# Reordering the start of a transformer block: the third tile's norm first, transposes inside a half step, scale groups inside the K steps

## The chip, the core and the metric

The kernel runs on one core of one Trainium2 chip. The metric is the device time of one execution in microseconds (us), measured in several executions; medians are quoted. A profile is one execution recorded instruction by instruction. Its span is 1.7 to 2 us shorter than the quoted time of an execution, so only differences are compared across the two.

TensorE does the matmuls. VectorE and ScalarE do elementwise work and copy results out of PSUM, the memory that matmuls write. GpSimd does a few small operations. The sync queue issues the loads, which 16 DMA engines carry out. In profile lines PE is TensorE, PEld its weight loads, DVE VectorE, ACT ScalarE, POOL GpSimd and SP the sync queue; L280 is a line of the kernel, x6 a count, `out<-in` names tiles: `pk` the K accumulators, `pq` those of q, `pt` transposes, `pm` scale factors, `big` the modulated rows.

## The reference

One block of a diffusion transformer, with 2 batches of 256 rows and a width D of 1152. All inputs are bf16.

```python
mod = (_silu(c) @ w_mod).reshape(B, 6, 1, D)
shift_a, scale_a, gate_a, shift_m, scale_m, gate_m = [mod[:, i] for i in range(6)]
h = _layernorm(x, axis=-1) * (1 + scale_a) + shift_a
qkv = (h @ wqkv).reshape(B, N, 3, H, Dh)
# ... softmax attention with two heads, output projection wo ...
x = x + gate_a * a
h2 = _layernorm(x, axis=-1) * (1 + scale_m) + shift_m
m = _gelu(h2 @ w_fc1) @ w_fc2
return x + gate_m * m
```

The change concerns the first 26 us: the first layer norm, `scale_a`, and the K part of `qkv`.

## The kernel before

The 512 rows are four tiles of 128: tiles 0 and 1 are batch 0, tiles 2 and 3 are batch 1. The width is nine chunks of 128. For each chunk k, TensorE transposes the normalized rows (`transpose_x`). VectorE scales batch 0's half on its way out of PSUM and ScalarE scales batch 1's half (`both`, called modulation here). Six matmuls of 512 columns then add chunk k into six K accumulators (`k_step`). The factors `scale_a` of a pair of chunks come from a scale group: 9 matmuls of 2 columns per chunk, then one add of 1.0 on VectorE (`scale_add`).

```python
def both(pt, k):
    for b, e in enumerate("da"):                 # d: VectorE, a: ScalarE
        modulate(pt, 0, k, b, b * N, e)
# ... statistics of tile 0 on ScalarE, of tile 1 on VectorE; both rstd ...
act_stats(2)                                     # tile 2: two passes on ScalarE
stats_piece(3, 0)                                # tile 3: three pieces on VectorE
stats_piece(3, 1)
norm1(1, 0, CUT)
norm1(0, 0, CUT)
pt_a = transpose_x([0, 1], BT[0])
fill(1)                                          # a matmul nobody reads: keeps TensorE busy
stats_piece(3, 2)
pool_eps(3)
pool_rsqrt(3, 4)
act_mean_eps(2)
act_root(2)
root_exp(2, 3)
pm0, pm1 = [scale_group(k, k + 1, acc_tile) for k in range(2)]
nc.vector.tensor_scalar_mul(hT0[:, 0, 0:N], pt_a[:, 0, :], pm0[:, 0, 0:1])
# ... batch 0's other modulation ...
norm1(3, 0, CUT)
norm1(2, 0, CUT)
fill(1)
k_step(0, 0, N)                                  # batch 0's half steps
k_step(1, 0, N)
pt_c = aux_tile([P, 2, N], "pt", BF16)
transpose_x([0, 1], [3], pt_c, 1)
transpose_x([0, 1], [2], pt_c, 0)
modulate(pt_c, 0, 0, 1, 0, "d")
modulate(pt_c, 1, 1, 1, 0, "a")
# ...
k_step(0, N, T)                                  # batch 1's first half step
# ... steps 1 and 2 ...
for k in range(3, KD):
    split = 2 if k == 5 else 0
    k_step(k, 0, T, 0, split)                    # the step's first `split` matmuls
    if k in (3, 5, 7):
        k1 = min(k + 3, KD)
        scale_add(scale_group(k + 1, k1), k + 1, k1)
    if k < KD - 1:
        both(transpose_x([k + 1], range(NT)), k + 1)
    k_step(k, 0, T, split)                       # the rest of the step
```

After step 8 come three more K panels (`k_panel`), then q, the scores, v, the output projection, and the two big matmuls fc1 and fc2.

Of the kernel before, what the change touches and what calls it, by code (L numbers as in the profile page):

```python
# [9 lines left out]
BF16 = mybir.dt.bfloat16  # L10
# [9 lines left out]
def kernel(  # L20
# [12 lines left out]
    B, N, D = x.shape  # L33
# [3 lines left out]
    P = 128  # L37
    T = B * N
    NT = T // P
    TPB = N // P  # L40
    KD = D // P
# [3 lines left out]
    NPD = D // PW  # L45
# [14 lines left out]
    def acc_tile(shape, name, dt=FP32):  # L60
        return psum.tile(shape, dt, name=name, tag="acc", bufs=6)

    def aux_tile(shape, name, dt=FP32):
        return psum.tile(shape, dt, name=name, tag="aux", bufs=2)
# [127 lines left out]
    def stats_piece(t, j):  # L192
        nc.vector.bn_stats(stats1[t][:, j, :], x_sb[:, t, j * PW:(j + 1) * PW])
        if j == NPD - 1:
            nc.vector.bn_aggr(mv1[:, t, :], stats1[t][:].rearrange("p a b -> p (a b)"))
# [8 lines left out]
    def act_stats(t):  # L204
        for f, dst in ((ACT.Identity, dsum), (ACT.Square, dsq)):
            nc.scalar.activation(
                sink[:], x_sb[:, t, :], f, bias=x_sb[:, t, 0:1], scale=-1.0,
                accum_out=dst[:, t:t + 1],
            )
# [22 lines left out]
    def norm1(t, c0, c1):  # L232
        nc.vector.tensor_scalar(
            xns[t][:, c0:c1], x_sb[:, t, c0:c1], mv1[:, t, 0:1], rstd1[:, t:t + 1],
            op0=ALU.subtract, op1=ALU.mult,
        )
# [4 lines left out]
    def scale_group(k0, k1, tile_of=aux_tile):  # L241
        pm = tile_of([P, k1 - k0, B], "pm")
        for j in range(k0, k1):
            if j == 0:
                nc.tensor.matmul(pm[:, 0, :], ones_row[:], ones_row[:, 0:B], start=True, stop=False)
            for k in range(KD):
                nc.tensor.matmul(
                    pm[:, j - k0, :], w_scale_a[:, k, j * P:(j + 1) * P], sT[:, k, 0:B],
                    start=(k == 0 and j > 0), stop=(k == KD - 1),
                )  # L250
        return pm

    def scale_add(pm, k0, k1, eng="d"):
        if eng == "a":
            nc.scalar.activation(scale_a[:, k0:k1, :], pm[:], ACT.Identity, bias=ones[:])
        else:
            nc.vector.tensor_scalar_add(scale_a[:, k0:k1, :], pm[:], 1.0)

    def transpose_x(ks, ts, pt=None, j0=0):
        if pt is None:  # L260
            pt = aux_tile([P, len(ks), len(ts) * P], "pt", BF16)
        for j, t in enumerate(ts, j0):
            for i, k in enumerate(ks):
                nc.tensor.transpose(pt[:, i, j * P:(j + 1) * P], xns[t][:, k * P:(k + 1) * P], ident[:])
        return pt

    def modulate(pt, i, k, b, j0, eng):
        dst, src, sc = hT0[:, k, b * N:(b + 1) * N], pt[:, i, j0:j0 + N], scale_a[:, k, b:b + 1]
        if eng == "d":
            nc.vector.tensor_scalar_mul(dst, src, sc)  # L270
        else:
            nc.scalar.mul(dst, src, sc)
# [3 lines left out]
    def k_step(k, c0=0, c1=T, m0=0, m1=KM1):  # L276
        for m in range(m0, m1):
            if k == 0 and c0 == 0:
                pk[m] = acc_tile([P, T], "pk")
            nc.tensor.matmul(  # L280
                pk[m][:, c0:c1], w_k[:, k, m * P:(m + 1) * P], hT0[:, k, c0:c1],
                start=(k == 0 and c0 == 0), stop=(k == KD - 1), skip_group_check=True,
            )
# [30 lines left out]
    CUT = 4 * P  # L314
    BT = [range(b * TPB, (b + 1) * TPB) for b in range(B)]

    def both(pt, k):
        for b, e in enumerate("da"):
            modulate(pt, 0, k, b, b * N, e)

    def fill(n):
        for _ in range(n):
            nc.tensor.matmul(pwarm[:], zeros[:, 0:P], zeros[:], start=True, stop=True)

    def pool_eps(t):
        nc.gpsimd.tensor_scalar_add(mv1[:, t, 1:2], mv1[:, t, 1:2], LN_EPS)

    def pool_rsqrt(t0, t1):
        nc.gpsimd.tensor_tensor(
            rstd1[:, t0:t1], mv1[:, t0:t1, 1:2].rearrange("p t o -> p (t o)"),  # L330
            neg_half[:, 0:t1 - t0], op=ALU.pow,
        )

    def act_root(t):
        nc.scalar.activation(rstd1[:, t:t + 1], dsq[:, t:t + 1], ACT.Ln, bias=dm2[:, t:t + 1], scale=1.0 / D)

    def root_exp(t0, t1):
        nc.scalar.activation(rstd1[:, t0:t1], rstd1[:, t0:t1], ACT.Exp, scale=-0.5)

    def act_mean_eps(t):  # L340
        act_sq_mean(t)
        nc.gpsimd.tensor_scalar_add(dm2[:, t:t + 1], dm2[:, t:t + 1], LN_EPS)
        act_mean(t)
# [7 lines left out]
    nc.scalar.activation(rstd1[:, 1:2], mv1[:, 1, 1:2], ACT.Ln, bias=eps_t[:], scale=1.0)  # L351
    root_exp(0, 2)
    act_stats(2)
    stats_piece(3, 0)
    stats_piece(3, 1)
    norm1(1, 0, CUT)
    norm1(0, 0, CUT)
    pt_a = transpose_x([0, 1], BT[0])
    fill(1)
    stats_piece(3, 2)  # L360
    pool_eps(3)
    pool_rsqrt(3, 4)
    act_mean_eps(2)
    act_root(2)
    root_exp(2, 3)
    pm0, pm1 = [scale_group(k, k + 1, acc_tile) for k in range(2)]
    nc.vector.tensor_scalar_mul(hT0[:, 0, 0:N], pt_a[:, 0, :], pm0[:, 0, 0:1])
    nc.vector.tensor_copy(scale_a[:, 0:1, :], pm0[:])
    scale_add(pm1, 1, 2)
    modulate(pt_a, 1, 1, 0, 0, "d")  # L370
    norm1(3, 0, CUT)
    norm1(2, 0, CUT)
    fill(1)
    k_step(0, 0, N)
    k_step(1, 0, N)
    pt_c = aux_tile([P, 2, N], "pt", BF16)
    transpose_x([0, 1], [3], pt_c, 1)
    transpose_x([0, 1], [2], pt_c, 0)
    modulate(pt_c, 0, 0, 1, 0, "d")
    modulate(pt_c, 1, 1, 1, 0, "a")  # L380
    norm1(0, CUT, D)
# [13 lines left out]
    k_step(2, 0, N)  # L395
    k_step(2, N, T)
    for k in range(3, KD):
        split = 2 if k == 5 else 0
        k_step(k, 0, T, 0, split)
        if k in (3, 5, 7):  # L400
            k1 = min(k + 3, KD)
            scale_add(scale_group(k + 1, k1), k + 1, k1)
        if k < KD - 1:
            both(transpose_x([k + 1], range(NT)), k + 1)
        k_step(k, 0, T, split)
    for m in range(KM1):
        k_evac(m)
# [386 lines left out]
    for gi, (n, t, c0, cw) in enumerate(groups):  # L794
# [3 lines left out]
        for kk in range(KF):  # L798
            j, r = divmod(n * KF + kk, 27)
# [55 lines left out]
```

## Time and profile before

The time before was 243.84 us (three runs, 243.69 to 244.43). From the page of the kernel before, the busy time of TensorE, and then, in 40 equal slices of the span, the busy tenths of the DMA engines and the rate:

```profile
PE 236.7 (98%) x1699; PEld 144.9 (60%) x1699; DVE 91.2 (38%) x193; ACT 60.0 (25%) x121; POOL 28.1 (12%) x47
...
DMA  6999999997579999239999999999300000000000
GB/s 210 318 317 294 378 367 391 389 392 241 124 252 399 387 382 182 47 58 334 392 390 392 345 326 302 273 326 289 94 20 16 20 16 16 19 18 17 27 23 16
```

TensorE is nearly always busy, and for the first 50 us the DMA engines are busy too, so either might set the pace there. The chain of waits, followed back from the last instruction, gives one candidate. Columns: start us, us, what ("issue" is time in which nothing that the profile shows was waited for).

```profile
18.62 1.66 SPq L129
...
20.32 12.40 DMA w_q<-in_wqkv_dram
32.72 0.05 issue
32.77 5.35 PE pq L522 x24
```

q's first matmul started when the first load of `w_q` landed, at 32.72 us. The waits of TensorE from 8 to 36 us (who waited, for what, us in total, times, longest) are these three:

```profile
PE pm L247 <- DMA w_scale_a<-in_w_mod_dram: 0.5, 1, 0.5
PE pk L280 <- DVE big L270: 0.4, 1, 0.4
PE pq L522 <- DMA w_q<-in_wqkv_dram: 0.2, 1, 0.2
```

The first is the wait for the first scale factors, the second the wait before batch 1's first K matmul, and the third the wait before q. The timeline around step 4 (first two lines) and around steps 7 and 8 shows what the change moves in the loop (start us, us, engine, line, operation, out<-in, shapes, count, idle before):

```profile
17.68 0.39 PE L264 MATMUL pt<-ident,xn 128*128 128x128 bf16 x4
17.91 1.89 PE L280 MATMUL pk<-big,w_k 128*128 128x512 bf16 x8
...
22.74 0.37 PE L247 MATMUL pm<-sT,w_scale_a 128*128 128x2 bf16 x9
...
22.97 0.38 PE L264 MATMUL pt<-ident,xn 128*128 128x128 bf16 x4
...
23.14 0.16 DVE L257 TENSOR_SCALAR scale_a<-pm 128x2 f32<-128x2 f32 x1 [1.20 <-PE pm L247]
23.19 2.75 PE L280 MATMUL pk<-big,w_k 128*128 128x512 bf16 x12
23.41 0.35 DVE L270 TENSOR_SCALAR big<-pt,scale_a 128x256 bf16<-128x256 bf16 x1
...
23.79 0.47 ACT L272 ACTIVATE big<-pt,scale_a 128x256 bf16<-128x256 bf16 x1 [1.34 <-DVE big L270]
```

Step 4's matmuls follow the transposes ahead of them (4 x 56 ns) without a hole. For step 8, the scale group and the transposes come first. Then the six matmuls of step 7 and the six of step 8 run as one row of 12, 2.75 us, while the add, VectorE and ScalarE prepare step 8 behind them.

**How holes are measured below.** From start to start, a matmul of 512 columns takes 216 ns in this trace when the next one is ready, one of 256 columns 109 ns, a transpose 56 ns, and a 2-column matmul 25 ns. A hole is the time from start to start above that pace. By this measure batch 1's first K matmul had a hole of 0.60 us before it, and q's first one of 0.32 us.

### The profile page before, as it was taken

How to read it: one execution, taken by the hardware profiler on the slowest of the kernel's cores; microseconds unless marked ns; L12 is line 12 of the kernel's file. 1: busy time of each engine (PE TensorE's matmuls, PEld its weight loads, DVE VectorE, ACT ScalarE, POOL GpSimd, SP SyncE). 2: the span in 40 equal slices, each digit the busy share in tenths (PEclk: the TensorE clock that was granted, in tenths of full speed). 3: DMA queues.
4: the chain of work that ended last, by engine and by line, in shares of the span. 5: the costliest groups of instructions: out<-in, count | busy, mean ns of one | idle time of the engine just before them, and what ended most of it. 6: DMA issues, size and time to landing. Idle time of an engine off the chain costs nothing.

```text
span 242.2 us, 3991 instructions
## 1 busy us (share of the span) xinstructions
PE 236.7 (98%) x1699; PEld 144.9 (60%) x1699; DVE 91.2 (38%) x193; ACT 60.0 (25%) x121; POOL 28.1 (12%) x47
## 2 busy tenths in 40 slices
PE   8899999999999999999999999999999999999994
PEld 5685444465667665888844444444666566656674
DVE  4742442318316678831001999960010000000001
ACT  6633322307215032771422233322000000000000
POOL 2200000001300333200000000001121111111111
PEclk9999999999999999999999999999999999999999
DMA  6999999997579999239999999999300000000000
GB/s 210 318 317 294 378 367 391 389 392 241 124 252 399 387 382 182 47 58 334 392 390 392 345 326 302 273 326 289 94 20 16 20 16 16 19 18 17 27 23 16
DMA packets 48781, 53.29 MB, mean 220 GB/s; under 512 B 9587, under 2 KB 36475, under 8 KB 48763
## 3 DMA queue, kind: packets, MB, share of 16 engines
q1 hardware_dynamic: 41312, 50.14, 62.4%
q10 hardware_dynamic: 6939, 1.71, 4.8%
q0 software_dynamic: 512, 1.19, 1.7%
q8 instruction: 13, 0.21, 0.4%
q14 instruction: 5, 0.04, 0.0%
HBM read 50.14 MB, written 1.19 MB: 212 GB/s over the span
## 4 chain that ended last, share of the span: by engine, by line
PE 85%; SPq 8%; DMA 5%; issue 0%; DVE 0%; DVEq 0%
PE pacc L744 29%; PE pacc L800 29%; PE pq L522 7%; PE pacc L691 7%; PE pacc L600 7%; SPq L104 5%; DMA w_q<-in_wqkv_dram 5%; PE pa L640 2%; PE ps_s L557 2%; PE pn L417 1%; SPq L107 1%; SPq L129 1%; SPq L86 1%; PE pg L499 0%; DVE tmp L806 0%
## 5 line engine op out<-in xcount | busy, mean ns | idle before, releaser
L744 PE MATMUL pacc<-hT,w_f 128*128 128x256 bf16 (+1 forms) x432 | 70.5, 326 | 0.0
L800 PE MATMUL pacc<-w_f,gT 128*128 128x384 bf16 (+2 forms) x468 | 70.5, 314 | 0.0
L800 PEld LDWEIGHTS <-gT 128*128 128x128 bf16 x468 | 44.4, 98 | 26.2
L744 PEld LDWEIGHTS <-w_f 128*128 128x128 bf16 x432 | 42.2, 98 | 27.6
L806 DVE TENSOR_TENSOR tmp<-pacc,gate 128x384 f32<-128x384 f32 (+2 forms) x13 | 6.8, 526 | 65.6 <-PE pacc L800 56.8
L776 ACT ACTIVATE gT<-pacc 128x512 bf16<-128x512 f32 x24 | 14.3, 597 | 32.6 <-PE pacc L744 32.6
L470 DVE SCALAR_TENSOR_TENSOR part<-w_gate_m,s,part 128x1152 f32<-128x1152 bf16 x16 | 21.3, 1408 | 0.0
L522 PE MATMUL pq<-hT,w_q 128*128 128x512 bf16 x81 | 17.8, 379 | 0.2 <-DMA w_q<-in_wqkv_dram 0.2
L691 PE MATMUL pacc<-w_o,big 128*128 128x384 bf16 x108 | 17.9, 326 | 0.0
L808 POOL TENSOR_TENSOR o_sb<-tmp,x 128x384 bf16<-128x384 f32 (+1 forms) x12 | 11.7, 972 | 53.8 <-DVE tmp L806 53.8
L600 PE MATMUL pacc<-w_v,hT 128*128 128x384 bf16 x108 | 17.7, 326 | 0.0
L600 PEld LDWEIGHTS <-hT 128*128 128x128 bf16 x108 | 10.5, 98 | 7.1 <-issue 0.3
L691 PEld LDWEIGHTS <-big 128*128 128x128 bf16 x108 | 10.4, 98 | 7.2 <-issue 0.4
L522 PEld LDWEIGHTS <-w_q 128*128 128x128 bf16 x81 | 7.8, 98 | 9.8 <-DMA w_q<-in_wqkv_dram 0.7
L280 PE MATMUL pk<-big,w_k 128*128 128x256 bf16 (+1 forms) x72 | 13.2, 325 | 0.4 <-DVE big L270 0.4
L697 POOL TENSOR_TENSOR x<-tmp,x_sb 128x384 f32<-128x384 f32 x8 | 7.3, 913 | 27.6 <-DVE tmp L696 27.6
L468 DVE TENSOR_SCALAR part<-w_gate_m,s 128x1152 f32<-128x1152 bf16 x2 | 1.5, 816 | 22.3 <-DMA w_gate_m<-in_w_mod_dram 22.3
L280 PEld LDWEIGHTS <-w_k 128*128 128x128 bf16 x72 | 6.8, 97 | 4.2 <-issue 0.8
L492 POOL DMA_DIRECT2D gates_dram<-nat_v x2 | 1.1, 534 | 67.5 <-DVE nat_v L490 67.5
L765 ACT ACTIVATE gT<-pacc 128x512 bf16<-128x512 f32 x12 | 6.5, 598 | 9.0 <-PE pacc L744 9.0
L513 POOL DMA_DIRECT2D gates_dram<-nat x4 | 2.3, 582 | 49.3 <-DVE nat L510 48.7
L173 PE MATMUL pwarm<-zeros 128*128 128x256 f32 x18 | 6.7, 541 | 1.2 <-DVE eps_t L93 1.2
(102 smaller groups left out, 164.8 us busy)
## 6 DMA issues: line engine op xcount, KB each, us to landing
w_f<-in_w_fc_dram SPq DMA_DIRECT2D x12, 864.0 KB, 14.8
w_f<-in_w_fc_dram SPq DMA_DIRECT2D x3, 1728.0 KB, 7.9
w_f<-in_w_fc_dram SPq DMA_DIRECT2D x2, 2592.0 KB, 17.2
w_gate_a<-in_w_mod_dram SPq DMA_DIRECT2D x3, 864.0 KB, 12.1
w_v<-in_wqkv_dram SPq DMA_DIRECT2D x3, 864.0 KB, 13.8
w_o<-in_wo_dram SPq DMA_DIRECT2D x3, 864.0 KB, 14.0
w_shift_m<-in_w_mod_dram SPq DMA_DIRECT2D x3, 864.0 KB, 6.6
w_scale_m<-in_w_mod_dram SPq DMA_DIRECT2D x3, 864.0 KB, 12.8
```

The lines of the kernel that those rows point to most:

```text
L104: nc.sync.dma_start(w_k[:, k0:k1, c0:c1], wqkv_v[:, k0:k1, D + c0:D + c1])
L280: nc.tensor.matmul(pk[m][:, c0:c1], w_k[:, k, m * P:(m + 1) * P], hT0[:, k, c0:c1], start=(k == 0 and c0 == 0), stop=(k == KD - 1), skip_g ...
L470: nc.vector.scalar_tensor_tensor(part[:, b, :], wg[:, k, :], s32[:, k, b:b + 1], part[:, b, :], op0=ALU.mult, op1=ALU.add,)
L522: nc.tensor.matmul(pq[m][:], w_q[:, k, m * P:(m + 1) * P], hT[:, k, :], start=(k == 0), stop=(k == KD - 1), skip_group_check=True,)
L600: nc.tensor.matmul(pacc[:], hT[:, k, t * P:(t + 1) * P], w_v[:, k, pnl * PW:(pnl + 1) * PW], start=(k == 0), stop=(k == KD - 1),)
L691: nc.tensor.matmul(pacc[:], aT[:, k, t * P:(t + 1) * P], w_o[:, k, c0:c1], start=(k == 0), stop=(k == KD - 1),)
L697: (nc.gpsimd if pool_add else nc.vector).tensor_tensor(x1[:, t, c0:c1], tmp[:], x_sb[:, t, c0:c1], op=ALU.add)
L744: nc.tensor.matmul(dst, w_f1[m // KD][:, k, ml * P:(ml + 1) * P], hT[:, k, c0:c1], start=start, stop=(k == KD - 1), **kw,)
L776: nc.scalar.activation(gT[:, m, :], pacc[:], ACT.Gelu_apprx_tanh)
L800: nc.tensor.matmul(pacc[:], gT[:, kk, t * P:(t + 1) * P], w_f2[j][:, r, c0 - n * PW:c0 - n * PW + cw], start=(kk == 0), stop=(kk == KF - 1),)
L806: nc.vector.tensor_tensor(tmp[:], pacc[:], gate_m[:, b, c0:c0 + cw], op=ALU.mult)
L808: (nc.vector if last else nc.gpsimd).tensor_tensor(o_sb[:], tmp[:], x1[:, t, c0:c0 + cw], op=ALU.add)
```

## The change

The intent has two parts. The first is to bring tile 3's norm forward into VectorE's wait for the scale factors, and to put tile 2's transposes between the matmuls of the second half step, so that some matmuls cover batch 1's first modulation. The second is to put every scale group from step 3 on inside its K step (after two of its matmuls) and behind the transposes of the next chunk.

```diff
-    stats_piece(3, 0)
-    stats_piece(3, 1)
+    for j in range(NPD):
+        stats_piece(3, j)
+    pool_eps(3)
+    pool_rsqrt(3, 4)
     norm1(1, 0, CUT)
     norm1(0, 0, CUT)
     pt_a = transpose_x([0, 1], BT[0])
-    fill(1)
-    stats_piece(3, 2)
-    pool_eps(3)
-    pool_rsqrt(3, 4)
     act_mean_eps(2)
     act_root(2)
     root_exp(2, 3)
+    norm1(3, 0, CUT)
     pm0, pm1 = [scale_group(k, k + 1, acc_tile) for k in range(2)]
     ... cut ...
-    norm1(3, 0, CUT)
     norm1(2, 0, CUT)
+    pt_c = aux_tile([P, 2, N], "pt", BF16)
+    transpose_x([0, 1], [3], pt_c, 1)
     fill(1)
     k_step(0, 0, N)
-    k_step(1, 0, N)
-    pt_c = aux_tile([P, 2, N], "pt", BF16)
-    transpose_x([0, 1], [3], pt_c, 1)
+    k_step(1, 0, N, 0, 2)
     transpose_x([0, 1], [2], pt_c, 0)
+    k_step(1, 0, N, 2)
     ... cut ...
     for k in range(3, KD):
-        split = 2 if k == 5 else 0
+        split = 2 if k % 2 else 0
         k_step(k, 0, T, 0, split)
-        if k in (3, 5, 7):
+        pt = transpose_x([k + 1], range(NT)) if k < KD - 1 else None
+        if k % 2:
             k1 = min(k + 3, KD)
             scale_add(scale_group(k + 1, k1), k + 1, k1)
-        if k < KD - 1:
-            both(transpose_x([k + 1], range(NT)), k + 1)
+        if pt is not None:
+            both(pt, k + 1)
         k_step(k, 0, T, split)
```

## The prediction

> **What bounds it now.** By the chain of waits: from 0.7 to 32.7 us the chain holds no arithmetic, only the sync queue issuing weight loads and then the first w_q load, issued at 20.32 us, landed 12.40 us later, at 32.72 us. From 32.77 to 239.0 us it is TensorE alone. The loads are back to back: the window table gives 290 to 390 GB/s from 8 to 51 us. (The Trainium skill, "DMA: Bandwidth & Descriptors", Where 436 GB/s comes from, puts the limit for loads from HBM at about 358; this trace reaches 390 from 38 to 51 us.) The change doesn't touch their order.
>
> TensorE isn't far behind: its last K matmul starts at 32.23 us, so q could start at about 32.45; it starts at 32.77 (waits: 0.16 us of modelled idle, put down to w_q). So TensorE already has about 0.3 us of slack.
>
> **What the change moves** (nothing is new; one 512-column filler matmul, 0.22 us, goes).
> 1. Tile 3's third statistics piece and aggregate (0.5 + 0.24 us on VectorE) precede the norms of tiles 1 and 0, which start about 7.8 instead of 7.28 us; their transposes slip from 8.07 to about 8.6. Free: the scale matmuls after them wait for w_scale_a until 9.24 us.
> 2. Tile 3's norm (0.36 us) runs in VectorE's wait for those matmuls (0.89 us). Tile 2's norm ends about 10.9 instead of 11.17 us. Its transposes go behind 8 of the 12 first K matmuls; the other 4 (0.44 us) cover the modulation. Batch 1's first K matmul (0.44 us of idle before it) starts at 11.75 instead of 12.20 us. Gain there about 0.45 us.
> 3. Scale groups go inside steps 3 and 7, transposes ahead of them. TensorE's work is the same, but the modulations now follow the group: adding one 0.16, VectorE 0.35, then ScalarE 0.47 us (always after VectorE's in the timeline), with hand-overs about 1.2 us; 4 matmuls (0.87 us) and, except before step 8, 4 transposes (0.22 us) cover it. Estimate: new holes of 0.1 to 0.2 us before steps 4 and 6, 0.35 before step 8, which give back most of the 0.45.
>
> **On the critical path: nothing.** Whether TensorE arrives at q 0.4 us earlier or not, w_q lands at 32.72 us. Later loads have slack (second w_shift_a half: lands 37.59 us, needed at 37.97).
>
> **Prediction.** 243.75 us, 243.3 to 244.2 (the three runs before spread over 0.7). Faster by over 2% 0.005, within 0.99, slower 0.005.
>
> **What would show it.** (1) Tile 0/1 transposes near 8.6 us, first K matmul still at 10.1. (2) Batch 1's first K matmul near 11.75. (3) Holes before steps 4, 6, 8, longest before 8. (4) q's first matmul again at 32.75 ± 0.15 us, released by w_q, TensorE's wait there larger by what the head gained.
>
> **What would make it wrong.** w_q landing earlier in the changed kernel, or in executions without a profile, so that TensorE sets q's start: up to 0.4 us gain. A later fast clock: matmuls are 427 ns apart until about 6.0 us and 216 after. The Trainium skill ("TensorE: Matmul & The Clock Gate", Part 1) says that the default state is throttled and a busy window of about 3.4 us releases it, with free phase; this trace agrees[...]. Holes in steps 3 to 7 over 0.7 us in sum would make it slower by the excess.

## The result, and the profile after

The changed kernel took 244.33 us (four runs, 244.13 to 244.87) against 243.79 us before (243.69 to 244.43). The ratio is 1.002, 95% interval 0.9996 to 1.0045. A ratio is the mean time of one kernel's runs over that of the other's of the same rounds, so it is not quite the ratio of the medians quoted. The difference is 0.5 us and lies inside the 2% that counts as the same, but it has the opposite sign to the forecast's small gain, and it lies just outside the range (244.2 at most).

From the chain of waits of the changed kernel (start us, us, what), the part that answers to the one above:

```profile
24.80 0.48 ACT big L272
25.28 0.04 issue
25.32 1.46 PE pk L280 x6
...
33.07 0.38 PE pk L309
33.45 5.18 PE pq L522 x24
```

The load of `w_q` is gone from the chain: it landed at 31.85 us, 0.87 us earlier than in the profile before. TensorE's own work leads into q, whose first matmul started at 33.28 us, 216 ns after the last panel matmul (the chain counts it only from the end of that matmul's record, 33.45 us). In front of that stands step 8, which waited for ScalarE. TensorE's waits from 8 to 36 us:

```profile
PE pt L264 <- DVE xn L233: 0.5, 1, 0.5
PE pk L280 <- ACT big L272: 0.3, 1, 0.3
PE pm L247 <- DMA w_scale_a<-in_w_mod_dram: 0.3, 1, 0.3
```

The first line is the transposes of tiles 0 and 1, which wait for their norms. The wait for `w_q` is gone. The one for batch 1's modulation has fallen below what the list shows: by the measure of holes it is 0.17 us, with 0.27 us before tile 2's transposes, against 0.60. A wait of the K matmuls for ScalarE is new. The timelines of TensorE around steps 4 and 6, and then of steps 7 and 8, show how it arises:

```profile
17.57 0.39 PE L264 MATMUL pt<-ident,xn 128*128 128x128 bf16 x4
18.06 1.89 PE L280 MATMUL pk<-big,w_k 128*128 128x512 bf16 x8
...
21.32 0.39 PE L264 MATMUL pt<-ident,xn 128*128 128x128 bf16 x4
21.80 1.89 PE L280 MATMUL pk<-big,w_k 128*128 128x512 bf16 x8
```

```profile
23.53 0.39 PE L264 MATMUL pt<-ident,xn 128*128 128x128 bf16 x4
...
23.75 0.37 PE L247 MATMUL pm<-sT,w_scale_a 128*128 128x2 bf16 x9
...
23.98 1.02 PE L280 MATMUL pk<-big,w_k 128*128 128x512 bf16 x4
24.15 0.16 DVE L257 TENSOR_SCALAR scale_a<-pm 128x2 f32<-128x2 f32 x1 [2.06 <-PE pm L247]
24.35 0.35 DVE L270 TENSOR_SCALAR big<-pt,scale_a 128x256 bf16<-128x256 bf16 x1
...
24.80 0.47 ACT L272 ACTIVATE big<-pt,scale_a 128x256 bf16<-128x256 bf16 x1 [2.19 <-DVE big L270]
...
25.32 1.02 PE L280 MATMUL pk<-big,w_k 128*128 128x512 bf16 x4 [0.32 <-ACT big L272]
```

The row of 12 matmuls is broken. Four matmuls (0.87 us of pace) stand behind the scale group, while group, add, VectorE and ScalarE take 1.35 us in series, from the end of the last group matmul's turn on TensorE (23.98 us, when the next matmul starts) to step 8's start (25.32 us). The hole is 0.48 us. The same chain leaves 0.26 us each before steps 4 and 6, where four transposes (0.22 us) help to cover it: step 4 starts at 18.06 us, and its transposes' turn ended at 17.80.

A sum from trace times shows where the 0.51 us between the two starts of q (32.77 and 33.28 us) came from:

| term | us |
|---|---|
| first K matmul later (10.22 against 10.07 us; the first `w_scale_a` load landed at 9.35 against 9.20 us) | +0.15 |
| from first K matmul to batch 1's first (1.87 against 2.13 us) | -0.26 |
| holes before steps 4, 6, 8 (0.26 + 0.26 + 0.48, against 0.05 before step 6) | +0.95 |
| hole before q for `w_q` (none against 0.32) | -0.32 |
| sum | +0.52 |

### The profile page after: what moved, and what is told of

The parts are those of the page before. It is cut to its first block, busy times and chain, and to the rows that moved or that the text cites. A ratio compares the mean times of both kernels' runs of the same rounds, so it can differ in the third digit from the quotient of the medians.

```text
span 242.7 us, 3978 instructions
## 1 busy us (share of the span) xinstructions
PE 236.4 (97%) x1687; PEld 144.8 (60%) x1698; DVE 91.5 (38%) x193; ACT 60.2 (25%) x121; POOL 28.1 (12%) x47
## 4 chain that ended last, share of the span: by engine, by line
PE 92%; DMA 2%; ACT 2%; DVE 1%; issue 1%; SPq 1%; ACTq 0%; DVEq 0%
PE pacc L800 29%; PE pacc L744 29%; PE pacc L691 7%; PE pacc L600 7%; PE pq L522 7%; PE pk L280 4%; PE pk L309 2%; DMA x_sb<-in_x_dram 2%; PE pa L640 2%; PE ps_s L557 2%; PE pn L417 2%; ACT sink L206 1%; PE pt L264 1%; PE pm L247 1%; ACT big L272 1%
```

## The experiments

Two theories stood first. Theory T: TensorE's own chain sets the start of q, and the new holes made the loss. Rival D: the landing of `w_q` sets the start of q, as the prediction held, and the 0.5 us is an accident of loads that landed later. In the table, "K to panel" is the time from the first K matmul to the first matmul of the panels after step 8. It holds nearly all of what the change moves, and leaves out when the first load happened to land. The first two rows are the profiles above. "before" is the median of the kernel before in the same rounds. The experiments ran in three jobs on three chips (e1 to e4; e5, e6, e7 and e9; e8, e10, e11 and e12), so across jobs only the distances to before are compared.

The last two columns account for the time. fc1's first matmul starts 65.2 to 65.3 us after q's in eleven of the fourteen profiles; it is 65.5 in e4, 65.9 in e5 and 66.2 in e7. In the thirteen profiles whose execution's time is on record (all but the first before), that time is 145.95 to 146.03 us more than fc1's start. So how much of a gain or loss in the head reaches the end can be read at fc1's start.

| run | us, median | before | ratio (95% interval) | K to panel | holes before 4 / 6 / 8 | first `w_q` landed | q starts | fc1 starts |
|---|---|---|---|---|---|---|---|---|
| before | 243.79 | - | - | 15.71 | - / 0.05 / - | 32.72 | 32.77 | 98.01 |
| after | 244.33 | 243.79 | 1.002 (0.9996 to 1.0045) | 16.39 | 0.26 / 0.26 / 0.48 | 31.85 | 33.28 | 98.55 |
| e3_before | 243.72 | 243.85 | 0.9993 (0.9977 to 1.0008) | 15.71 | - / 0.05 / - | 31.01 | 32.41 | 97.65 |
| e1_head | 243.68 | 243.85 | 0.999 (0.9973 to 1.0006) | 15.42 | - / 0.05 / - | 31.75 | 32.60 | 97.88 |
| e2_loop | 244.70 | 243.85 | 1.003 (1.0013 to 1.0047) | 16.66 | 0.26 / 0.26 / 0.48 | 31.45 | 33.23 | 98.55 |
| e4_group_first | 243.85 | 243.85 | 0.9996 (0.9981 to 1.0012) | 15.55 | 0.05 / 0.05 / 0.27 | 30.73 | 32.33 | 97.87 |
| e5_dd | 243.85 | 243.72 | 0.9992 (0.9964 to 1.0021) | 15.58 | - / - / 0.17 | 30.60 | 32.16 | 98.08 |
| e6_step7 | 244.14 | 243.72 | 1.0006 (0.9979 to 1.0034) | 16.14 | 0.26 / 0.26 / 0.05 | 31.88 | 32.91 | 98.16 |
| e9_after | 244.48 | 243.72 | 1.0022 (0.9991 to 1.0053) | 16.20 | 0.26 / 0.26 / 0.48 | 30.47 | 33.03 | 98.26 |
| e7_nogroups | 244.22 | 243.72 | 1.001 (0.9978 to 1.0043) | 14.69 | see text | 31.41 | 31.86 | 98.04 |
| e10_nogroups_hold | 242.79 | 243.72 | 0.9963 (0.9944 to 0.9982) | 15.50 | see text | 31.93 | 32.43 | 97.67 |
| e8_head_hold | 243.67 | 243.72 | 0.9995 (0.998 to 1.001) | 15.61 | - / 0.05 / - | 31.36 | 32.40 | 97.63 |
| e11_before_hold | 243.71 | 243.72 | 0.9997 (0.9983 to 1.0011) | 15.70 | - / 0.05 / - | 32.02 | 32.70 | 97.93 |
| e12_head_hold_dd | 243.57 | 243.72 | 0.9994 (0.998 to 1.0007) | 15.58 | - / - / - | 31.95 | 32.40 | 97.63 |

### e1_head: the first part alone

The loop is put back as it was before; the rest is the changed kernel.

```diff
-        split = 2 if k % 2 else 0
+        split = 2 if k == 5 else 0
         k_step(k, 0, T, 0, split)
-        pt = transpose_x([k + 1], range(NT)) if k < KD - 1 else None
-        if k % 2:
+        if k in (3, 5, 7):
             ... group and add as before ...
-        if pt is not None:
-            both(pt, k + 1)
+        if k < KD - 1:
+            both(transpose_x([k + 1], range(NT)), k + 1)
```

> The first part of the change alone (tile 3 ahead, tile 2's transposes inside the second half step); the loop over steps 3 to 8 as before. Theory T (TensorE's own chain sets the start of q, the new holes before steps 4, 6 and 8 made the loss): no hole over 0.1 us before steps 4, 6, 8; the wait at batch 1's first K matmul about 0.45 us above the pace instead of 0.6; q could start at about 32.2 us; 0.2 to 0.5 us faster than before, less in executions where w_q lands late. Rival D (the landing of w_q sets the start of q, and the 0.5 us of the change came from loads that landed later): within 0.1 us of before.

The holes before steps 4 and 8 are gone, and K to panel is 15.42 us, 0.29 us shorter than before. The first K matmul came late in this profile (10.52 us, because the first `w_scale_a` load landed at 9.64 us; it comes 0.87 us after that load in all profiles but e3_before's), so q started at 32.60 us and not at 32.2. The median is 0.17 us below before, with an interval that holds 1.000. So the first part does shorten TensorE's head by 0.3 us, but the clock hardly shows it. Where that gain goes is the question of the last group of runs.

### e2_loop: the second part alone

The head is as before, and the loop is the changed one.

```diff
-        split = 2 if k == 5 else 0
+        split = 2 if k % 2 else 0
         k_step(k, 0, T, 0, split)
+        pt = transpose_x([k + 1], range(NT)) if k < KD - 1 else None
         ... group and both() behind the transposes, as in the change ...
```

> The loop part alone; the head as before. Theory T: holes of about 0.26, 0.26 and 0.48 us before steps 4, 6 and 8, q starts at about 33.4 us, 0.6 to 0.95 us slower than before. Rival D: within 0.1 us of before.

All three holes are there to within 0.01 us. The waits of TensorE from 8 to 36 us hold the old one of the head and the new one before step 8:

```profile
PE pk L280 <- DVE big L270: 0.4, 1, 0.4
PE pk L280 <- ACT big L272: 0.3, 1, 0.3
```

K to panel is 16.66 us, 0.95 longer than before, and the kernel is 0.85 us slower by the medians, the only slower run here whose interval excludes 1.000. The loop part alone makes the loss. Rival D falls: TensorE started q 1.8 us after `w_q` had landed.

### e3_before: the kernel before, profiled again

No edit.

> The kernel before once more, for a second profile and the noise of the comparison. Both theories: ratio 1.000 within 0.001. Theory T: q's first matmul starts at 32.4 to 32.8 us; the landing of the first w_q load moves by up to 1 us between executions (it was 32.72 us before and 31.85 us in the changed kernel), and q follows it only where it lands after 32.4 us. Rival D: it lands near 32.7 us again and q starts with it.

`w_q` landed at 31.01 us, and q started at 32.41 us on TensorE's own time. The waits of TensorE from 8 to 36 us have shrunk to one line:

```profile
PE pk L280 <- DVE big L270: 0.4, 1, 0.4
```

So the wait for `w_q`, on which the prediction rested, belonged to one execution. Over the fourteen profiles the first `w_q` load landed between 30.47 and 32.72 us, and the latest of all was the one in the profile before. No other profile has TensorE waiting for it. e9_after repeats the other side.

### e4_group_first: the group ahead of the transposes

```diff
         k_step(k, 0, T, 0, split)
-        pt = transpose_x([k + 1], range(NT)) if k < KD - 1 else None
         if k % 2:
             k1 = min(k + 3, KD)
             scale_add(scale_group(k + 1, k1), k + 1, k1)
-        if pt is not None:
-            both(pt, k + 1)
+        if k < KD - 1:
+            both(transpose_x([k + 1], range(NT)), k + 1)
```

> The whole change, but in steps 3, 5 and 7 the scale group goes ahead of the four transposes, as step 5 of the kernel before had it. Theory T (what counts is how much matmul work stands between the group and the next step): the transposes cover 0.2 us more, so holes of about 0.05, 0.05 and 0.25 us instead of 0.26, 0.26 and 0.48; 0.6 us faster than the changed kernel, from 0.3 us faster than before to the same. A rival in which the place of the group inside the step alone makes the holes: as the changed kernel, 0.5 us slower than before.

The holes are 0.05, 0.05 and 0.27 us, as expected from 0.22 us more cover. K to panel is 15.55 us, and the median equals the one before. The groups still stand inside steps 3, 5 and 7 here, so the place inside the step isn't what costs. What counts is how much TensorE work stands between a group and the step that needs it. The change took the transposes (0.22 us) out of that stretch in all three steps, and in steps 3 and 7 two of the six matmuls (0.43 us) as well, since the group used to stand ahead of all six. The sums agree with the holes. The chain of 1.35 us less 4 matmuls (0.87) and twice 4 transposes (0.44) leaves 0.04 us, and 0.05 was measured before steps 4 and 6. Less 4 matmuls and 4 transposes it leaves 0.26, and 0.27 was measured before step 8.

### e5_dd: a shorter chain

```diff
     def both(pt, k):
-        for b, e in enumerate("da"):
+        for b, e in enumerate("dd"):
             modulate(pt, 0, k, b, b * N, e)
```

> The whole change, with both modulations of a step from step 4 on given to VectorE (one after the other, 0.35 us each) instead of VectorE and then ScalarE (0.47 us, which starts only after VectorE's). Theory C (the holes are the serial chain scale group, add, VectorE, ScalarE, less the matmuls that cover it): the chain is 0.15 to 0.2 us shorter, so holes of about 0.08, 0.08 and 0.3 us instead of 0.26, 0.26 and 0.48; 0.5 us faster than the changed kernel, the same as before within 0.2 us. If the holes come from the hand-over of the weights or of the group's accumulator on TensorE instead, they stay and the time stays 0.5 us above before.

The holes before steps 4 and 6 vanish and the one before step 8 falls to 0.17 us. From e5_dd's timeline, step 7's last four matmuls and step 8's first six in one row:

```profile
22.94 0.37 PE L247 MATMUL pm<-sT,w_scale_a 128*128 128x2 bf16 x9
23.17 2.49 PE L280 MATMUL pk<-big,w_k 128*128 128x512 bf16 x10
```

That is about 0.3 us less (0.15 to 0.2 was expected) for the same order of TensorE work, with only ScalarE's turn taken out, so the holes are the serial chain. The median is 0.63 us below the changed kernel's of the same job (244.48 us, e9_after). In the changed kernel, ScalarE's wait for VectorE's modulation is the longest wait of ScalarE from 12 to 26 us:

```profile
ACT big L272 <- DVE big L270: 10.7, 8, 2.4
```

All eight of ScalarE's modulations start after VectorE's half has ended. No line of the kernel asks for this; the wait stands in the built program. The Trainium skill has a reason for keeping the two apart ("PSUM — Partial Sum Buffer", PSUM bank collisions raise a hardware error): two engines may not access the same bank and quadrant of PSUM at once, even at different columns, and the hardware doesn't hold one back. Both halves lie in one PSUM tile. The traces agree with the order (every ScalarE half starts 0.03 to 0.10 us after VectorE's ends). No run here tried them together.

### e6_step7: step 7's group back in front

```diff
-        split = 2 if k % 2 else 0
+        split = 2 if k in (3, 5) else 0
```

> The whole change, but step 7's transposes and scale group go back ahead of its matmuls (as before); steps 3 and 5 as changed. Theory C: no hole before step 8 (six matmuls, 1.3 us, cover a chain of about 1.35 us less the hand-over; under 0.1 us), 0.26 us each before steps 4 and 6 as in the changed kernel; 0.4 us faster than the changed kernel, from the same as before to 0.2 us slower.

The hole before step 8 falls from 0.48 to 0.05 us and the other two stay. The median of 244.14 us lies between before and changed; its distance to the changed kernel of the same job (244.48) is 0.34 us. One thing was not expected: the scale group of step 5 waited 0.3 us for its `w_scale_a` load, which landed at 20.00 us. In eight of the fourteen profiles that load landed between 17.8 and 18.8 us, in the other six between 19.5 and 20.0 us.

### e9_after: the changed kernel again

No edit to the changed kernel.

> The changed kernel once more beside the others, on the same chip. Theory T: holes of 0.26, 0.26 and 0.48 us again, q 0.6 to 0.7 us later after the first K matmul than in the kernel before (22.37 us), not waiting for w_q; 0.4 to 0.7 us slower than before. Rival D (an accident of loads that landed later in the one profile): the two kernels within 0.2 us.

The three holes are the same to 0.01 us, `w_q` landed at 30.47 us and q started at 33.03 us. The median is 0.76 us above before; the interval of the ratio is wide (0.9991 to 1.0053), since one run of the kernel before in these rounds took 245.82 us, at the lowest granted clock of all (0.992). Without that run the ratio of the means would be 1.0028; it also lowers the ratios of e5, e6 and e7 by 0.0008. The gain of the first part differed, though: here batch 1's first K matmul came 1.59 us after the first K matmul, against 1.87 us in the first profile and 2.13 us before. In that first profile tile 2's rows landed at 7.42 us and held ScalarE's statistics back by 0.24 us; here they landed at 6.97 us.

### e7_nogroups: less TensorE work (wrong result)

The first part alone, and no scale groups from step 3 on. Chunks 4 to 8 use the factors of chunks 2 and 3, so the result is wrong.

```diff
-        ... scale_a[:, k, b:b + 1]
+        ... scale_a[:, k if k < 4 else 2 + k % 2, b:b + 1]
-        if k in (3, 5, 7):
-            k1 = min(k + 3, KD)
-            scale_add(scale_group(k + 1, k1), k + 1, k1)
```

> Wrong result on purpose: the first part of the change alone, and no scale groups from step 3 on (chunks 4 to 8 are scaled by the factors of chunks 2 and 3), which takes 45 matmuls of about 25 ns, 1.1 us, off TensorE. It measures the slack that the loads leave. If TensorE alone sets q's start, it moves from 22.08 to about 20.95 us after the first K matmul and the kernel is 1.1 us faster than the first part alone. Theory T with the landings seen so far (the first w_q load between 30.7 and 32.7 us, the first half of w_shift_a between 28.5 and 29.6): TensorE waits for one of these loads in most executions, and the gain is 0.3 to 0.8 us.

This was a miss, and the most useful run. q started at 31.86 us, 0.91 us earlier than in the profile before, and TensorE waited for neither `w_q` nor `w_shift_a` there. (Ahead of q it waited for `w_k` loads: the holes are 0.20 us before step 6 and 0.25 us before the first panel.) Yet the kernel was no faster than before: its median is 0.5 us higher, with an interval that holds 1.000. The gain vanished 66 us later. From e7_nogroups's waits of TensorE, and then of VectorE, around 93 to 100 us:

```profile
PE pacc L740 <- DVE hT L659: 0.8, 1, 0.8
```

```profile
DVE hT L659 <- DMA hT<-xn: 1.5, 1, 1.5
```

fc1's first matmul waited for VectorE's second modulation, which followed the first one directly, and the first one had waited for the DMA transpose of tile 1 into `hT`. This transpose was issued at 93.1 us and landed at 97.55 us:

```profile
L678 ACTq DMA_TRANSPOSE hT<-xn x1: 1315/1315/1315, 93.1 to 93.1; - x1
...
DMA to landing us min/median/max: 4.4/4.4/4.4
```

In e3_before it was issued at 93.7 and landed at 97.11 us. So an earlier issue did not bring an earlier landing. Theory F: the landing is held up by a load of `w_f1` that stands in front, and this second floor swallows what the head gains. The traces point to the first load of `w_f1`'s second tile. Tile 0's transpose was issued at 86.8 to 88.2 us and landed at 96.2 to 97.2 us in the ten profiles without the hold of the next section, each time within 0.9 us of that load's landing, and at 92.5 to 93.8 us in the four with the hold. e4_group_first and e5_dd met the same floor: tile 1's transpose landed 3.8 and 4.1 us after its issue, and q's early start (32.33 and 32.16 us) lost 0.3 and 0.7 us before fc1.

### e8, e10, e11, e12: the transposes freed from the load

All four hold the first load of `w_f1`'s second tile until tile 1's transpose has landed (the kernel already holds that tile's second load in this way).

```diff
+        first_load.setdefault("w_f1_1", load.ins)
     ...
-        nc.scalar.dma_start_transpose(hT[:, :, t * P:(t + 1) * P], xn2[:])
+        return nc.scalar.dma_start_transpose(hT[:, :, t * P:(t + 1) * P], xn2[:])
     ...
-            ln2_normalize(t, t % 2 == 1, BETWEEN.get(t, ()))
+            tr = ln2_normalize(t, t % 2 == 1, BETWEEN.get(t, ()))
+            if t == 1:
+                tc.add_manual_dep(first_load["w_f1_1"], tr.ins.name, WAIT_FOR, reason="transposes first")
```

e8 adds this to e1_head, e10 to e7_nogroups, e11 to the kernel before, and e12 to e1_head with `both` all on VectorE as in e5_dd.

For e10 the record expected:

> Wrong result on purpose: no scale groups from step 3 on, as the run without them, and the load held as above. Theory F: the transpose of tile 1 lands 2.5 to 3 us after its issue, so by about 96 us, and fc1 starts at about 96.9 us instead of 98.0; the gain of some 0.7 us at q, which vanished before fc1 in the run without the hold, now reaches the end: 0.8 to 1.2 us faster than before. Without a floor at the transposes: as the run without the hold, no faster than before.

The kernel without groups is now 0.93 us faster than before, with an interval clear of 1.000 (0.9944 to 0.9982). The same edit without the hold had gained nothing (e7, in another job; the two intervals overlap only from 0.9978 to 0.9982). The profiled execution was the slowest of the six (243.62 us): in it TensorE lost 1.2 us before step 6 and the first panel to late `w_k` loads (holes of 0.84 and 0.39 us), so K to panel is 15.50 us. That profile therefore doesn't show the gain itself. It shows that the wait before fc1 is gone, in part because q started 0.57 us later than in e7. But the transpose, issued at 93.7, landed at 96.92 us; with e7's landing fc1 would still have waited until about 98.04. From the timelines of TensorE from 96 to 99 us, e7_nogroups and then e10_nogroups_hold:

```profile
95.78 1.46 PE L687 MATMUL pacc<-w_o,big 128*128 128x384 bf16 x8
98.04 1.14 PE L740 MATMUL pacc<-hT,w_f 128*128 128x256 bf16 x9 [0.79 <-DVE hT L659]
```

```profile
95.72 2.11 PE L688 MATMUL pacc<-w_o,big 128*128 128x384 bf16 x12
97.67 1.58 PE L743 MATMUL pacc<-hT,w_f 128*128 128x256 bf16 x13
```

For e11:

> The kernel before with that load held, as a control. Theory F: before, TensorE and the transposes arrive at fc1 within 0.2 us of each other, so the hold alone gains 0 to 0.2 us. If the hold itself makes the kernel faster whatever the head does, it gains as much here as in the first-part-alone run.

The control gains nothing (0.9997). Before, TensorE and the transposes arrive at fc1 together, as e3_before shows: there the transpose landed at 97.11 us, and fc1 started at 97.65 us without a hole. (With the hold, in e11, it landed at 97.19 us, 3.2 us after its issue.)

For e8:

> The first part of the change alone, and the load of w_f1's second tile (first 384 columns) held until tile 1's DMA transpose has landed. Theory F (a second floor: fc1's first matmul needs the modulated transposes, whose landing is held up by that load; what the head gains is lost there): the transpose of tile 1 lands by 96.6 us instead of 97.1 to 97.6, no wait before fc1, which starts at 97.3 to 97.6 us; 0.3 to 0.5 us faster than before. Without such a floor the hold changes nothing: 0.1 to 0.3 us faster than before, as the first part alone.

This one missed on time: fc1 started at 97.63 us without a wait, but the median is only 0.05 us below before. K to panel was 15.61 us and not 15.42. The scale group of step 5 waited 0.21 us for its `w_scale_a` load, which landed late (19.53 us) in this execution. So a third place caps the head in some executions (in e12's profile too: 0.21 us, landed at 19.58).

For e12:

> Candidate for a version faster than both: the first part of the change, the loop as before with both modulations of steps 4 to 8 on VectorE, the load held. Theory C and F: the small hole before step 6 (0.05 us) goes; 0.3 to 0.6 us faster than before, at most 0.1 us better than the first part with the hold.

This is the lowest median of the versions with a right result: 243.57 us (243.43 to 243.90), 0.15 us below before, with an interval from 0.998 to 1.0007. But e1_head, without the hold, was as far below its own before (0.17 us), so no gain is shown. The effect of the floor needs the 1 us of e10 to be visible on the clock; the 0.3 us of the first part alone stays within the noise.

## Why the prediction was wrong

The range failed: 244.33 us measured, 244.2 us at most predicted. It was right that the kernel stays within 2%. Point by point:

1. **Tile 3's statistics first: right.** The transposes of tiles 0 and 1 moved from 8.07 to 8.59 us (predicted 8.6). It cost nothing: the scale group still waited for its load, which landed at 9.35 us, and the first K matmul came 0.15 us later for that reason. The later fast clock that the prediction feared did not matter either: the warm-up's last matmul started at 7.72 instead of 7.58 us, and TensorE then idled 0.49 us for the norms.
2. **Batch 1's first K matmul: right mechanism, gain of varying size.** Predicted was 0.45 us. Measured from first K matmul to batch 1's first, it was 0.26 us in the first profile and 0.54 us in the second. The forecast took tile 2's rows as landed in time. In the first profile they were not.
3. **The new holes: right mechanism, a term mis-sized. This step failed first.** The prediction said "new holes of 0.1 to 0.2 us before steps 4 and 6, 0.35 before step 8, which give back most of the 0.45". They measured 0.26, 0.26 and 0.48 us, 1.00 together, in every profile of the changed loop (after, e2_loop, e9_after), so they gave back nearly four times the first profile's gain of 0.26. (Even its own holes sum to 0.55 to 0.75 us, more than the 0.45 that they were to give back most of.) The term is the chain, "with hand-overs about 1.2 us". From the end of the last group matmul's turn on TensorE it is 1.35 us; from the add on it is 1.17 (24.15 to 25.32 us). What was left out is the time from that turn until the result is used, about 0.17 us: the next matmul starts 25 ns after the last group matmul, but VectorE's add starts 0.20 us after it, in every step of every profile that has a group in the loop. The Trainium skill has this ("TensorE: Matmul & The Clock Gate", Single matmul latency): a warm matmul of N columns takes about (398 + N)/2.4 ns, an estimate of 167 ns for N = 2. The trace is in line with it: the record lasts 163 ns (its end is modelled by the profiler), and the 0.20 us measured include the hand-over. Counting a matmul by its start-to-start pace is right for TensorE's own time and wrong for whoever waits for the result.
4. **"On the critical path: nothing": the second step that failed.** "Whether TensorE arrives at q 0.4 us earlier or not, w_q lands at 32.72 us" took one execution's landing time for a property of the kernel. It was the latest landing of fourteen. In the other thirteen profiles TensorE's own chain starts q, e3_before among them, so the 0.3 us of slack that the prediction counted on isn't there. It would not have been enough either: the changed kernel's TensorE reached q at 33.28 us, after even the landing at 32.72. The prediction's own list of what would make it wrong named both things, an earlier landing and holes above 0.7 us in sum, but gave them too little weight.
5. **A floor that wasn't seen.** There is a limit from the DMA, but it stands before fc1 and not before q. It caps gains (e7 against e10; 0.3 and 0.7 us in the profiles of e4 and e5) and does nothing to stop losses: the second part's 0.95 us shows as 0.85 (e2_loop). That the first part brings 0.3 us in TensorE's head and at most 0.2 us on the clock is not shown to come from this floor. In e1's profile fc1 lost less than 0.1 us there, and the hold did not help (e8). What those two profiles show instead are late `w_scale_a` loads (9.64 us in e1, 19.53 us in e8).

Left open: why the landing of a load differs by 1 to 2 us between executions (the first `w_q` load 30.47 to 32.72 us, the fourth `w_scale_a` load early or late by about 1.2 us); no experiment touched it. And the loss of the changed kernel as a whole, 0.54 and 0.76 us by the medians, stands on two sets of runs whose single intervals still reach 1.000. Its sign is hardly in doubt: all ten runs of the changed kernel (244.13 us and more) lie above 28 of the 37 runs of the kernel before. Clear of noise in themselves are the loop part alone (e2_loop) and the holes in the traces.

## What to carry to other kernels

Before reordering, write down the chain that the consumer waits for, including the latency of the last producer, and count how much independent work stays between producer and consumer; moving the transposes from behind a small group to in front of it took 0.22 us of cover away in each of three places, and moving the group behind two matmuls another 0.43 us in two of them. A wait for a load that one profile shows at the end of a chain may be that execution's accident: profile the same kernel twice before calling a stage bound by it. When TensorE is shortened and nothing comes of it, look for the next place where it meets a load, and test it by freeing that load: gains are capped there, while losses pass through.

## What the Trainium skill lacked or had wrong

- "DMA: Bandwidth & Descriptors" (Where 436 GB/s comes from) puts the limit for loads from HBM at about 358 GB/s per core. Only a note in another section of the page ties that figure to both cores of an HBM domain streaming at once. This kernel runs on one core, which before moved 391 GB/s from 38 to 51 us, nearer to the 425 that the page's table gives for 16 MB.
- The same page has no figure for how far the landing of one load moves between executions of the same program. The fourteen profiles show 30.47 to 32.72 us for the first `w_q` load, 2.25 us apart.
- The same page gives a bandwidth for DMA transposes but no latency behind other loads. Tile 1's transpose took 3.3 to 4.4 us from issue to landing in the ten profiles without the hold, and 3.2 us with the load held (e8, e10, e11, e12).
- "TensorE: Matmul & The Clock Gate" (Part 4) gives about 275 ns for a 128x128 transpose in a kernel. The records here last 219 ns (their ends are modelled), and in a row follow each other at 56 ns, which is what counts for TensorE's time.
